# Transposing the column softmax weights by DMA instead of on TensorE, with a new written order of the pieces

## The chip, the cores and the metric

The kernel runs on one core of a Trainium2 chip. The metric is the device time of one execution in microseconds (us); lower is better. Three runs of the kernel before took 217.58, 217.84 and 218.04 us, a median of 217.84 us.

The core's engines are named as in the profile: PE is TensorE (matrix products; PEld is its weight load), DVE is VectorE, ACT is ScalarE, POOL is GpSimd, SP is SyncE, which here does nothing but issue DMAs. SBUF is the on-chip memory that all engines work from; PSUM is the small memory that PE writes its results to.

## What is computed

There are 8 batches `b` of 8 heads. For each head there are 512 rows of x and 32 rows of a state, all of 64 numbers. Attention goes both ways over one matrix of scores, and a two-layer network with a squared ReLU follows on the 4352 resulting rows:

```python
scores = scale * np.matmul(x, state.transpose(0, 1, 3, 2))     # softmax over the 32 states
xread  = np.matmul(a, state)
scores2 = scale * np.matmul(state, x.transpose(0, 1, 3, 2))    # softmax over the 512 rows
sread  = np.matmul(a2, x)
x = np.concatenate([xread, sread], axis=2)   # then (B*S, H*D) = (4352, 512)
r = np.maximum(x @ w_in, 0.0)                # w_in: 512 x 2048
out = (s * (r * r) + b) @ w_out              # w_out: 2048 x 512
```

The column softmax weights of the title are `a2`: for each state row, its weights over the 512 rows of x.

## The kernel before, in words

**The order is written out by hand.** `ORDER` (line 15) is a list of some 740 words. Each word is a piece: a name that the table `pieces` (line 724) maps to a function, and its arguments. The loop at line 735 calls them one by one, and each engine carries out its own instructions in exactly that order, under a manual schedule; semaphores between engines are put in by the framework where one piece needs another's data or buffer. A letter at the end of a word names the engine for its elementwise work: `A` is ACT, `V` is DVE, `G` is POOL. So `s.0.8.2.V` squares two row blocks of batch 0 on DVE, and `At.2.G` runs on POOL.

**Attention of a batch b.** `x.b` loads x as fp16 (POOL issues the DMA), `xT` transposes it on DVE in blocks of 32, `T` forms the scores on PE. For the row softmax, `U`, `mu`, `D`, `E1`, `z`, `At`, `A` (DVE, ACT, and POOL for some of the `At` and `D`) give the weights `A`. For the column softmax, `keep` saves the scores of some batches in SBUF, `nm` and `nms` take the maximum, `E2` the exponentials and their sums (ACT, two pieces per batch), and `a2` (line 395, DVE) divides: a reciprocal of the sums and two multiplications, into the tile a2 of 128 x 1024 fp16. All 128 partitions are state rows there.

**The transpose.** To sum over the rows of x, these weights must lie with the rows of x on the partitions. `aps` (line 405) does that with eight 128 x 128 transposes on PE into PSUM, and `a2T` (line 411) copies them to SBUF, seven times on ACT and once on DVE (batch 5). `V` (line 414) multiplies them by `xn`, a second copy of x in another layout that POOL loads (`load_xn`, line 193, four DMAs per batch), and `srd` puts the result into `srdT`. `V` runs for the batches 3, 4, 5 with 2, 6 with 0, 7, 1. Tiles: a2 has one buffer, a2T two, xn two.

**The network.** For the x rows, `M` multiplies state and w_in (PE), `Mc` copies that to SBUF (ACT, some on DVE), and `l` (line 489) is the first layer: two matmuls of 512 columns on PE and the ReLU on ACT. `s`, `sh`, `ssr` square (line 484), on ACT, DVE or POOL. The second layer of batches 0 and 1 is `L` (line 512: four matmuls per quarter `q`), with `out` for bias and store. Batches 2 to 7 use seven products of half-size blocks instead of eight: `S` (line 576) forms sums of blocks, `P` (line 597) is half of a product (eight matmuls of 256 columns), `ev` (line 611) takes a PSUM bank's state over into the output tiles `osx0` and `osx1` on DVE, and `put` (line 619) stores them through SP. The two osx tiles have one buffer each, so the first `ev` on one of them waits until the stores of the batch before have landed. The state rows go through `lsr`, `ssr`, `S_sr`, `P_sr` and `ev_sr` at the end.

**Queues.** SP issues the stores in the order of the words `out` and `put`; POOL issues all loads, between its elementwise pieces.

**The two pieces that the change takes out, and the loop that calls all pieces:**

```python
for c in range(SCH):
    transp(aps[:, SCH * g + c], at[b]["a2"][:, g, P * c : P * c + P])
...
copy(e, sm(b, "a2T", [P, NG * SCH, P], FP16, apool, 2), at[b]["aps"])
...
for line in ORDER:
    for word in line.split():
        name, *args = word.split(".")
```

Of the kernel before, what the change touches and what calls it, by code (L numbers as in the profile page):

```python
# [11 lines left out]
FP16 = mybir.dt.float16  # L12
# [70 lines left out]
def kernel(  # L83
# [321 lines left out]
    def at_aps(b):  # L405
        at[b]["aps"] = aps = blocks(two_banks(f"aps_{b}", FP16), 0)
        for g in range(NG):
            for c in range(SCH):
                transp(aps[:, SCH * g + c], at[b]["a2"][:, g, P * c : P * c + P])

    def at_a2T(b, e):
        copy(e, sm(b, "a2T", [P, NG * SCH, P], FP16, apool, 2), at[b]["aps"])
# [97 lines left out]
    ops_t = {}  # L510

    def layer2(tag, rr, q):
        if q == 0:
            ops_t[tag, rr] = ps_o.tile([P, DM], FP32, name=f"ops_{tag}_{rr}", tag="po")
        for f in range(4 * q, 4 * q + 4):
            nc.tensor.matmul(  # L516
                ops_t[tag, rr],
                G_t[tag][:, f, P * rr : P * rr + P],
                w_out_f(f),
                start=(f == 0),  # L520
                stop=(f == NKF - 1),
            )
# [74 lines left out]
    def product(b, u):  # L597
# [3 lines left out]
        first, last = bank not in [p[0] for p in PRODUCTS[:n]], bank not in [p[0] for p in PRODUCTS[n + 1 :]]  # L601
        lhs = block(b, *lhs) if lhs else fast(b, "S3")
        for k in range(4 * h, 4 * h + 4):
            w = fast_w[rhs][:, k] if isinstance(rhs, str) else w_block(*rhs)(k)
            for rr in range(2):
                mm(
                    fast(b, bank)[:, rr], lhs[:, k, P * rr : P * rr + P], w,
                    start=(first and k == 0 and rr == 0), stop=(last and k == NKF // 2 - 1 and rr == 1), skip=True,
                )
# [50 lines left out]
    def bias_sum(q):  # L660
        if q == 0:
            cps_t.append(two_banks("cps")[:, 0, :])
# [106 lines left out]
```

## Time and profile before

| what | value |
|---|---|
| median of three runs (lowest, highest) | 217.84 us (217.58, 218.04) |
| span of the profiled execution, first to last instruction | 215.7 us |
| mean granted TensorE clock | 0.992 |
| busy PE / PEld / DVE / ACT / POOL | 205.8 / 130.0 / 179.6 / 158.0 / 86.9 us |
| transposing pieces on PE (`aps`, 64 matmuls) | 4.9 us busy |
| copies out of PSUM (`a2T`) | 7.1 us on ACT (7), 0.7 us on DVE (1) |
| DMA traffic | 22.43 MB in 23658 packets |

The profile is of one execution. "Busy" is the time in which at least one instruction of the engine is under way, and consecutive matmuls overlap, so that a group's busy time is more than what it costs between its neighbours. A row of a group gives the line, engine, operation, the tile written, the tiles read, the shape, the number of instructions, their busy time, the mean duration of one, and the idle time before them with what ended it. The chain is followed back from the last instruction: at each step to what released it. The timeline gives start and length of merged instructions. The time of 217.84 us covers the span and what lies around it, 2.1 us here.

### The profile page before, as it was taken

How to read it: one execution, taken by the hardware profiler on the slowest of the kernel's cores; microseconds unless marked ns; L12 is line 12 of the kernel's file. 1: busy time of each engine (PE TensorE's matmuls, PEld its weight loads, DVE VectorE, ACT ScalarE, POOL GpSimd, SP SyncE). 2: the span in 40 equal slices, each digit the busy share in tenths (PEclk: the TensorE clock that was granted, in tenths of full speed). 3: DMA queues.
4: the chain of work that ended last, by engine and by line, in shares of the span. 5: the costliest groups of instructions: out<-in, count | busy, mean ns of one | idle time of the engine just before them, and what ended most of it. 6: DMA issues, size and time to landing. Idle time of an engine off the chain costs nothing.

```text
span 215.7 us, 4829 instructions
## 1 busy us (share of the span) xinstructions
PE 205.8 (95%) x1955; PEld 130.0 (60%) x1955; DVE 179.6 (83%) x277; ACT 158.0 (73%) x260; POOL 86.9 (40%) x94
## 2 busy tenths in 40 slices
PE   7489999999999999999999999999999999999992
PEld 2134343344444448767677677677766777888881
DVE  2997899999998799969998999999986874593661
ACT  4598886899899788799999887779768475734300
POOL 8554126445093033157437057007223308916400
PEclk9969999999999999999999999999999999999999
DMA  6999998127849719523900939608902600440045
GB/s 153 175 207 206 196 206 146 41 63 106 137 106 140 133 20 171 68 50 64 162 24 2 187 112 115 82 17 145 221 8 46 144 11 0 102 97 0 5 147 145
DMA packets 23658, 22.43 MB, mean 104 GB/s; under 512 B 4436, under 2 KB 17492, under 8 KB 23636
## 3 DMA queue, kind: packets, MB, share of 16 engines
q0 software_dynamic: 16848, 12.52, 41.3%
q1 hardware_dynamic: 5504, 8.66, 14.9%
q10 hardware_dynamic: 1284, 0.95, 1.7%
q8 instruction: 15, 0.25, 0.5%
q14 instruction: 7, 0.06, 0.1%
HBM read 25.72 MB, written 8.91 MB: 161 GB/s over the span
## 4 chain that ended last, share of the span: by engine, by line
PE 91%; DMA 3%; ACT 2%; POOL 1%; DVE 1%; issue 0%; POOLq 0%
PE hps L472 25%; PE opf_X L141 20%; PE ops L516 13%; PE opf_W L141 10%; PE opf_Y L141 5%; PE mps L141 5%; DMA w_in<-in_moe_w_in_dram 3%; PE hps_sr L472 3%; PE vps L141 2%; PE aps L141 2%; PE ops_sr_X L141 2%; PE T_None L141 2%; ACT M L156 1%; PE hph L141 1%; PE ops_sr_W L141 1%; PE dps L683 1%
## 5 line engine op out<-in xcount | busy, mean ns | idle before, releaser
L476 ACT ACTIVATE r<-hps 128x512 f16<-128x512 f32 x120 | 68.8, 603 | 25.6 <-PE hps L472 22.3
L472 PE MATMUL hps<-A,M 128*128 128x512 f16 x240 | 65.6, 380 | 0.1
L141 PEld LDWEIGHTS <-g 128*128 128x128 f16 x576 | 56.0, 98 | 15.2 <-issue 0.9
L472 PEld LDWEIGHTS <-M 128*128 128x128 f16 x240 | 21.4, 98 | 19.8 <-issue 6.0
L482 POOL TENSOR_TENSOR g<-r 128x1024 f16<-128x1024 f16 (+1 forms) x9 | 21.3, 2372 | 27.0 <-ACT r L476 22.8
L156 ACT CAST M<-mps 128x1024 f16<-128x1024 f32 x29 | 29.2, 1013 | 2.3 <-PE mps L141 1.9
L516 PE MATMUL ops<-w_out,g 128*128 128x512 f16 x128 | 30.7, 379 | 0.0
L197 POOL DMA_DIRECT2D xn<-in_x_dram x32 | 18.7, 604 | 14.8 <-PE vps L141 14.0
L141 PE MATMUL opf_X<-w_T,g 128*128 128x256 f16 x192 | 24.1, 273 | 0.0
L482 DVE TENSOR_TENSOR g<-r 128x1024 f16<-128x1024 f16 (+1 forms) x30 | 22.1, 754 | 1.6 <-ACT r L476 1.6
L586 DVE TENSOR_TENSOR g<-g 128x1024 f16<-128x1024 f16 (+1 forms) x31 | 22.1, 728 | 0.2
L516 PEld LDWEIGHTS <-g 128*128 128x128 f16 x128 | 12.4, 98 | 14.9 <-POOL g L482 0.2
L615 DVE SCALAR_TENSOR_TENSOR osx<-opf_X,sb_bc,bias_bc 128x512 f32<-128x512 f32 x18 | 13.3, 740 | 7.7 <-PE opf_X L141 7.4
L357 POOL TENSOR_TENSOR At<-E,rz 128x1024 f16<-128x1024 f16 x4 | 7.7, 1914 | 21.6 <-DVE rz L348 21.6
L480 ACT ACTIVATE g<-r 128x1024 f16<-128x1024 f16 (+1 forms) x11 | 15.8, 1444 | 0.2
L141 PE MATMUL mps<-w_in,stT 64*32 64x512 f16 x256 | 13.0, 397 | 1.6 <-DMA w_in<-in_moe_w_in_dram 1.3
L586 POOL TENSOR_TENSOR g<-g 128x1024 f16<-128x1024 f16 (+1 forms) x3 | 8.3, 2768 | 15.4 <-PE opf_X L141 8.1
L141 PE MATMUL opf_W<-w_out,g 128*128 128x256 f16 x96 | 12.4, 273 | 0.0
L141 PE MATMUL opf_W<-w_T,g 128*128 128x256 f16 x96 | 12.3, 273 | 0.0
L141 PE MATMUL opf_X<-w_out,g 128*128 128x256 f16 x96 | 12.1, 273 | 0.0
L141 PE MATMUL opf_X<-w_T,S 128*128 128x256 f16 x96 | 11.8, 273 | 0.0
L141 PE MATMUL opf_Y<-w_out,g 128*128 128x256 f16 x96 | 11.8, 273 | 0.0
(102 smaller groups left out, 310.4 us busy)
## 6 DMA issues: line engine op xcount, KB each, us to landing
out_dram<-osx SPq DMA_DIRECT2D x44, 128.0 KB, 2.4
xn<-in_x_dram POOLq DMA_DIRECT2D x32, 128.0 KB, 6.7
xh<-in_x_dram POOLq DMA_DIRECT2D x14, 256.0 KB, 5.2
w_in<-in_moe_w_in_dram POOLq DMA_DIRECT2D x8, 256.0 KB, 9.2
w_out<-in_moe_w_out_dram POOLq DMA_DIRECT2D x4, 512.0 KB, 13.3
out_dram<-osb SPq DMA_DIRECT2D x16, 64.0 KB, 1.9
out_dram<-osb SPq DMA_DIRECT2D x8, 128.0 KB, 2.4
xf<-in_x_dram SPq DMA_DIRECT2D x2, 256.0 KB, 3.7
```

Source lines behind the costliest of these rows:

```text
L141: return nc.tensor.matmul(out, lhsT, rhs, start=start, stop=stop, tile_position=tp, is_transpose=is_transpose, skip_group_check=skip,)
L156: (engine.copy if engine is nc.scalar else engine.tensor_copy)(out, in_)
L197: nc.gpsimd.dma_start(out=xn_t[b][32 * jh : 32 * jh + 32].rearrange("t h c d -> t h (c d)"), in_=x[b].rearrange("h (t jh c) d -> jh t h (c ...
L357: e.tensor_tensor(out, E1, over_n(rz), ALU.mult)
L472: nc.tensor.matmul(hps, lhsT, rhs, start=(i == 0), stop=(i == len(terms) - 1))
L476: nc.scalar.activation(R_t[tag, q][:, i], hps, AF.Relu)
L480: nc.scalar.activation(g, r, AF.Square)
L482: e.tensor_mul(g, r, r)
L516: nc.tensor.matmul(ops_t[tag, rr], G_t[tag][:, f, P * rr : P * rr + P], w_out_f(f), start=(f == 0), stop=(f == NKF - 1),)
L586: e.tensor_tensor(out, x, y, op)
L615: nc.vector.scalar_tensor_tensor(out, fast(b, name[0]), s_bc, out if plus else bias, ALU.mult, ALU.add)
L683: nc.tensor.matmul(dps, ones16[:, :P], ones16, start=True, stop=True)
```

## The change

- `aps` and `a2T` go. A piece `tr` takes their place: one DMA, issued by SP, that reads a2 and writes a2T transposed, from SBUF to SBUF, 256 KB.
- The head of the order (the first 60 words) is kept; all later pieces stand in a new order. The pieces are otherwise the same in kind and number.
- Engines of elementwise pieces are given out anew. POOL keeps one (`s.1.12.4.G`) of 24. ACT gets 26 squares of two blocks instead of 6, DVE 14 instead of 27; all `At`, `D`, `S` and `S_sr` go to DVE.
- `layer2`, `product` and `bias_sum` no longer need their quarters or halves in a fixed sequence: the first visit to a PSUM bank starts the sum and the last one stops it, counted by `visit`. The new order uses that (for instance `L.1.3.3` is the first of its bank, and `P.5.7` stands ahead of `P.5.6`).
- SP's queue, by the words of the new order: `out.0.0` to `out.0.3`, `tr.3`, `out.1.0`, `out.1.3`, `out.1.1`, `tr.4`, `out.1.2`, `tr.5`, the stores of batch 2, `tr.2`, the first stores of batch 3, `tr.6` between the two halves of `put.3.1`, `tr.0`, the stores of batch 4, `tr.7`, `tr.1`, then the stores of the batches 5 to 7.

```diff
-    def at_aps(b):
-        at[b]["aps"] = aps = blocks(two_banks(f"aps_{b}", FP16), 0)
-        for g in range(NG):
-            for c in range(SCH):
-                transp(aps[:, SCH * g + c], at[b]["a2"][:, g, P * c : P * c + P])
-
-    def at_a2T(b, e):
-        copy(e, sm(b, "a2T", [P, NG * SCH, P], FP16, apool, 2), at[b]["aps"])
+    def at_tr(b):
+        a2T = sm(b, "a2T", [P, NG * SCH, P], FP16, apool, 2)
+        nc.sync.dma_start_transpose(out=a2T, in_=at[b]["a2"].rearrange("p g s -> p (g s)"))
...
+    def visit(*key):
+        visits[key] = visits.get(key, 0) + 1
+        return visits[key]
...
     def layer2(tag, rr, q):
-        if q == 0:
+        v = visit("L", tag, rr)
+        if v == 1:
             ops_t[tag, rr] = ps_o.tile([P, DM], FP32, name=f"ops_{tag}_{rr}", tag="po")
...
-                start=(f == 0),
-                stop=(f == NKF - 1),
+                start=(v == 1 and f == 4 * q),
+                stop=(v == NKF // 4 and f == 4 * q + 3),
...
     def product(b, u):
...
-                    start=(first and k == 0 and rr == 0), stop=(last and k == NKF // 2 - 1 and rr == 1), skip=True,
+                    start=(v == 1 and k == 4 * h and rr == 0),
+                    stop=(v == visits_all and k == 4 * h + 3 and rr == 1), skip=True,
```

The words of the new order around the places that matter here:

```
tr.3 l.2.12 s.2.0.2.A s.2.2.2.A mu.4 V.3
...
ev.2.X4 S.3.2.1.V ev.3.X1 S.3.2.0.V x.7 s.4.2.2.A l.4.6 s.4.6.2.A z.5 P.3.2 l.4.1 nm.6 nms.6.V xn.6 P.3.5
l.4.0 turn.12.16.A s.4.0.2.A P.3.3 E2.6.1 l.4.8 l.4.14 E2.6.0 At.5.V put.2.0.0 ev.3.Y P.3.4
put.2.1.0 U.6 P.3.7 put.2.1.1 S.3.4.1.V ev.3.X2 nm.0 P.3.6 l.4.13 s.4.4.2.A M.5.1.1 A.5 tr.2 V.5.2
...
a2.0 P.4.12 ev.4.W2 P.5.0 s.5.14.2.A Mc.6.3.A l.6.11 mu.7 tr.0 s.6.2.2.V l.6.8 P.5.1 E2.7.0
l.6.0 ev.4.X4 V.6.0
...
P.5.10 a2.7 put.4.0.1 ev.5.X3 P.5.12 l.7.3 l.7.1 s.6.10.2.V s.6.12.2.A Mc.7.2.V S.6.3.0.V
put.4.1.0 P.5.13 l.7.0 put.4.1.1 tr.7 S.6.1.0.V l.7.8 V.7 l.7.5 a2.1 tr.1 s.7.2.2.V l.7.9 P.6.0
ev.5.W2 S.6.3.1.V l.7.10 P.6.1 P.6.3 ev.5.X4 S.6.1.1.V srd.7 l.7.6 put.5.0.0 S.6.2.1.V P.6.2 l.7.11
ev.6.X1 S.6.2.0.V l.7.7 P.6.4
```

More of the change, by code (lines that the diff above doesn't have):

```diff
@@ L508, in layer1_sr @@
         layer1("sr", f, [(w_in_f(k, f), srdT[:, k].rearrange("p n b -> p (n b)")) for k in range(NK)], B * Ns)
-    ops_t = {}
+    ops_t, visits = {}, {}
+    def visit(*key):
+        visits[key] = visits.get(key, 0) + 1
+        return visits[key]
     def layer2(tag, rr, q):
-        if q == 0:
+        v = visit("L", tag, rr)
+        if v == 1:
             ops_t[tag, rr] = ps_o.tile([P, DM], FP32, name=f"ops_{tag}_{rr}", tag="po")
@@ L600, in product @@
         bank, lhs, rhs = PRODUCTS[n]
-        first, last = bank not in [p[0] for p in PRODUCTS[:n]], bank not in [p[0] for p in PRODUCTS[n + 1 :]]
+        v, visits_all = visit("P", b, bank), 2 * sum(p[0] == bank for p in PRODUCTS)
         lhs = block(b, *lhs) if lhs else fast(b, "S3")
@@ L660, in bias_sum @@
     def bias_sum(q):
-        if q == 0:
+        v = visit("cps")
+        if v == 1:
             cps_t.append(two_banks("cps")[:, 0, :])
@@ L667, in bias_sum @@
                 cps[32 * c : 32 * c + 32, :], ones16[:, 0:32], w_out_f(f),
-                start=(f < 4), stop=(f >= NKF - 4), tp=(0, 32 * c),
+                start=(v == 1), stop=(v == NKF // 4), tp=(0, 32 * c),
             )
@@ L728 @@
         "E1": at_E1, "z": at_z, "At": at_At, "A": at_A, "nm": at_nm, "nms": at_nms, "E2": at_E2, "a2": at_a2,
-        "aps": at_aps, "a2T": at_a2T, "V": at_V, "srd": at_srd, "M": at_M, "Mc": at_Mc,
+        "tr": at_tr, "V": at_V, "srd": at_srd, "M": at_M, "Mc": at_Mc,
         "lh": layer1_half, "sh": square_half, "l": layer1_x, "s": square, "lsr": layer1_sr,
```

117 rows, old and new, of the table ORDER are left out of this document.

## The prediction

> **What bounds the kernel now.** I read the profile in this order: the page's busy times and slices, the chain that ended last, busy times by stage, then the timeline around the pieces that the change takes out. The page first, then the busy times by stage (start:end, length, then per engine the busy us and the instructions, TensorE clock, DMA share, GB/s):
>
> ```profile
> PE 205.8 (95%) x1955; PEld 130.0 (60%) x1955; DVE 179.6 (83%) x277; ACT 158.0 (73%) x260; POOL 86.9 (40%) x94
> ...
> PE   7489999999999999999999999999999999999992
> ...
> PE 91%; DMA 3%; ACT 2%; POOL 1%; DVE 1%; issue 0%; POOLq 0%
> ```
>
> ```profile
> 40.00:80.00 40.00, 40.00 (x323) 17.51 (x321) 37.09 (x49) 36.07 (x56) 13.94 (x21) 1.00 0.58 99
> 80.00:120.00 40.00, 40.00 (x425) 28.70 (x411) 36.78 (x58) 35.98 (x58) 18.79 (x17) 1.00 0.47 78
> 120.00:160.00 40.00, 40.00 (x450) 28.69 (x445) 38.33 (x59) 31.66 (x52) 13.25 (x18) 1.00 0.68 116
> 160.00:190.00 30.00, 30.00 (x309) 22.30 (x308) 20.04 (x31) 19.02 (x35) 14.06 (x7) 1.00 0.26 60
> ```
>
> The reader is to see that TensorE (PE) is never idle from 40 to 190 us, and is 91% of the chain: in this stretch only two things move the end, PE work added or removed, and a new wait of PE. DVE stands close behind: 37.09 + 36.78 + 38.33 = 112.2 of 120 us.
>
> The written order can be read as a clock. From the chain, a piece `l` (two matmuls of 512) costs PE 0.43 us, `P` (eight of 256) 0.87, one batch of `V` 0.57, `M` 0.44:
>
> ```profile
> 119.43 1.14 PE vps L141 x64
> ...
> 127.44 0.86 PE hps L472 x4
> ...
> 129.18 1.75 PE opf_X L141 x16
> ```
>
> Summed by such costs, the pieces from L.0.0.2 (starts at 35.3) to P.7.10 (201.9) make 166.6 us, which is what the trace has. So the PE pieces between two words of the new order give the time between them.
>
> **1. The transposes leave PE.** In the timeline a transposing piece starts at 104.42 and the next matmul at 104.88:
>
> ```profile
> 104.42 0.62 PE L141 MATMUL aps<-ident,a 128*128 128x128 f16 x8
> ...
> 104.88 0.59 PE L472 MATMUL hps<-A,M 128*128 128x512 f16 x2
> ```
>
> Its 0.62 us overlaps what follows; its net cost is 0.45 us (the eight pieces give 0.45 to 0.48). Eight go: **-3.6 us**, all of it on the bound engine. No other PE piece is added or removed.
>
> **2. The elementwise work.** Rows of the groups by shape (busy us, mean ns | idle before):
>
> ```profile
> L482 DVE TENSOR_TENSOR g<-r 128x1024 f16<-128x1024 f16 x27 | 18.6, 703 | 1.6 <-ACT r L476 1.6
> ...
> L156 ACT COPY a2T<-aps 128x1024 f16<-128x1024 f16 x7 | 7.1, 1015 | 0.0
> ...
> L480 ACT ACTIVATE g<-r 128x1024 f16<-128x1024 f16 x6 | 6.2, 1054 | 0.1
> ```
>
> ACT: 20 more squares of 1024 (+21.1), one fewer of 2048 (-1.9), seven a2T copies fewer (-7.1), two M copies fewer (2 x 1.01 = -2.0), five squares of 512 more (5 x 0.62 = +3.1): +13.2, from 158.0 to 171. DVE: At +4 (5.2), D +1 (1.2), M copies +2 (2.4), S +4 and one double (2.8 + 1.2), two more squares of 2048 (2.4), sums of the state rows +2 (0.9), 13 fewer squares of 1024 (-9.1), three small pieces fewer (-1.5 with the eighth a2T copy): +5.5, from 179.6 to 185. Both stay under PE's 202, so I cost them at nothing on the path; PE's own work is the cover. It is thin on DVE from 40 to 160: with two thirds of the 5.5 there, 115.8 us against 116.9 of PE (120 less seven transposing pieces); with all of it, 117.7. GpSimd loses about 43 us; nothing waited long for it.
>
> **3. The new wait.** V now waits for a DMA issued by SP; the trace of before has none from SBUF to SBUF. Call L the time from the end of a2 on DVE to a2T in place. The room for L is what PE has to do between a2 and V in the new order, less a2's 0.8 us (0.16 + 2 x 0.35):
> - V.7: P.5.12, l.7.3, l.7.1, P.5.13, l.7.0, l.7.8 = 3.5, room **2.7**.
> - V.0 (second batch of V.6.0): three P, three l and the batch of V.6 = 4.5, room **3.7**.
> - V.2 (second batch of V.5.2): on SP's queue tr.2 stands behind put.2.1.0 and put.2.1.1, which need ev.2.X4. From there to V.2 are six l, six P, one M and a batch, 8.8; less the eviction (0.75) and four issues (0.64 each) room 5.5.
> - V.3 and V.1 have about 7 (V.1 after tr.7 as well), V.4, V.5 and V.6 over 15.
>
> Nearest rows for L (KB each, us from issue to landing), and queue totals (packets, MB, share of 16 engines):
>
> ```profile
> out_dram<-osx SPq DMA_DIRECT2D x44, 128.0 KB, 2.4
> ...
> xf<-in_x_dram SPq DMA_DIRECT2D x2, 256.0 KB, 3.7
> ```
>
> ```profile
> q0 software_dynamic: 16848, 12.52, 41.3%
> ```
>
> Below: 2.4, a store of half the bytes. Above: the build splits the transpose into 64 tiles of 16 x 128, or 1024 rows of 256 bytes; GpSimd's packets took 0.413 x 16 x 215.7 / 16848 = 85 ns each, so 64 per engine are 5.4 us, and with 2.0 around them 7.4. I take 3.7, the row that has the same 256 KB on the same queue. So V.7 waits 1.0 us and the others nothing: **+1.0**.
>
> The Trainium skill (DMA: Bandwidth & Descriptors, Latency and other measured facts) gives 261 GB/s for a DMA transpose; by it the 256 KB move in an estimated 1.0 us, and added to those 2.0 L is 3.0 and V.7 waits 0.3. No run yet shows it.
>
> a2 has one buffer, so a2.1 waits for tr.7 to land; behind it on DVE stand s.7.2.2 and ev.5.W2. With L of 3.7 it lands as DVE gets there.
>
> **4. Output buffers.** The osx tiles have one buffer each: ev.6.X1 waits for the stores of put.5.0, which wait for ev.5.W2, and P.6.4 waits for ev.6.X1. The trace shows four issues and what followed:
>
> ```profile
> 164.40 2.94 SPq L624 DMA_DIRECT2D out_dram<-osx  x4
> ```
>
> From ev.5.W2 to P.6.4 the new order has four l and three P, 4.3 us; the way round needs 0.75 + 3 x 0.64 + 2.4 + 0.75 = 5.8, 1.5 too long. DVE may run ahead of its words, since ev.5.W2 needs only P.5.10, six us before. I take half: **+0.8** (bounds 0 and 1.5). tr.1 now stands ahead of put.5.0 on SP; its issue costs 0.5 to 1.9 us by SP's other issues, and is covered if it is under 1.2.
>
> **5. xn.2** needs V.4's buffer, and V.2 follows V.4's end by 9.3 us. In the trace of before the same load started 0.3 us after V.4 and landed 4.7 after its last issue at most: 6.9 with the issues. It is hidden; by the slowest row (7.7) it would be 0.5 late.
>
> ```profile
> 100.30 2.35 POOL L197 DMA_DIRECT2D xn<-in_x_dram  x4 [1.20 <-PE vps L141]
> ```
>
> **6. The rest.** The head is the same up to lh.0.4.1, and the last three products of the state rows end both orders: nothing, at most 0.9 either way for the small PE idles between 14 and 40 us (24.78 busy of 26).
>
> **Sum.** -3.6 + 1.0 + 0.8 = -1.8. The profiled span is 215.7 and gives 213.9; the median of the runs shown, 217.84, has 2.1 around that span, so 216.0.
>
> **Rivals.**
> - *Everything hidden* (0.15): L under 2.7 and DVE ahead of its words. 217.8 - 3.6 = 214.2. For it: from 40 to 190 the order of before left PE no idle at all, with the copies in the way from a2 to V. Against: the rooms above are the narrowest of the order.
> - *Slow transpose* (0.30), the one that ends slower: every us of L beyond 2.7 stops PE at V.7, beyond 3.7 at V.0 too, beyond 5.5 at V.2. With the 0.8 it outweighs the gain from L = 4.6. At 5.5: 2.8 + 1.8 + 0.8 = 5.4, 219.6; at 7.4: 4.7 + 3.7 + 1.9 + 0.8 = 11.1, 225.3. For it: the packet row; against: the row of the same bytes. An extreme of it, inside that chance with 0.04: the eight blocks of 128 x 128 go one after the other, each with the 1.9 us that the smallest store (64 KB) took, so L is over 10 and the time over 235. The Trainium skill (VectorE: DVE Perf Modes, The three transpose paths) speaks for this side: 1309 ns for one such block by DMA against 390 on TensorE; eight in a row are an estimated 10.5 us. The trace already differs from its TensorE figure, with 0.45 us for eight.
> - *DVE becomes the bound* (0.15): the 117.7 against 116.9, with pieces out of step: 1 to 3 us beyond the forecast, about 217.8. For it: DVE's 93% from 40 to 160. Against: GpSimd's pieces were slow (2 us each) and waited for others.
> - That the change does not do what it says is excluded by the build: eight transposes on SP, no aps on PE, one elementwise piece on GpSimd.
>
> **How the numbers follow.** Forecast 0.40, with 214.7 to 217.3 as its own range (L from 2.4 to 4.2, P.6.4 from 0 to 1.5). A measurement of this kernel can tell about 0.2% (0.4 us) from no change. Faster: 0.40 + 0.15 + a quarter of the DVE case = 0.58; same: half of the DVE case and a little of the slow one, 0.10; slower 0.32. The range goes from 213.8 (all hidden, and some of the early idles gone) to 220.8 (L of 5.9); above it lies about 0.15.
>
> **What would show it.** Right: no aps rows; PE idle only at V.7 (waiting for a2T) and before P.6.4, 1 us each; issue to landing of a2T near 3.7. Wrong: landing above 4.6; PE waits for DVE spread over 40 to 160 us; stores landing late behind the transposes.

## The result, and the profile after

| kernel | median, lowest to highest (us) | ratio to before, 95% interval | span (us), clock |
|---|---|---|---|
| before | 217.79 (217.58 to 218.04) | 1 | 215.7, 0.992 |
| after | 232.58 (232.42 to 232.78) | 1.067 [1.066, 1.069] | 230.6, 0.966 |

The change makes the kernel 14.8 us slower. The prediction, 216.0 us with a range to 220.8, had the wrong sign. Executions that took over 1.5% longer than the fastest one of their kernel are left out of all medians, ranges and ratios here, which concerns one kernel below.

The page of after: busy times, then PE by slice, the granted TensorE clock by slice, and the chain.

```profile
PE 207.5 (90%) x1891; PEld 128.4 (56%) x1891; DVE 182.9 (79%) x277; ACT 166.7 (72%) x275; POOL 42.9 (19%) x71
...
PE   7578599999999999799963999889999999999991
...
PEclk9889979999999999999996799999999999999998
...
PE 69%; DMA 10%; ACT 9%; DVE 7%; issue 1%; SPq 1%; POOL 1%; DVEq 0%; ACTq 0%; POOLq 0%
```

PE has 64 matmuls fewer, as it should, and yet it is busy for longer: behind the two deep holes (the fifth slice, and the 21st and 22nd; a slice is 5.8 us) the clock drops, and matmuls take longer. PE's share of the chain fell from 91% to 69%; DMA, ACT and DVE came in. The busy times by stage (PE, PEld, DVE, ACT, POOL, then clock, DMA share, GB/s) show that the row of full PE stages has broken:

```profile
80.00:120.00 40.00, 37.51 (x384) 24.94 (x383) 35.32 (x54) 34.80 (x57) 3.54 (x7) 1.00 0.54 80
120.00:160.00 40.00, 33.85 (x312) 22.93 (x306) 31.24 (x46) 27.41 (x41) 4.59 (x8) 0.91 0.50 79
```

DVE, which the prediction feared as the next bound, has more idle time there, not less: 31.24 busy of 40, against 38.33 before. So the loss is waits, not work. The waits of after (total us, times, longest) name them:

```profile
DVE U L327 <- ACT Ts L323: 6.8, 2, 4.1
PE vps L140 <- DMA a2T<-a: 4.5, 1, 4.5
...
DVE U L327 <- ACT E L389: 4.2, 2, 2.6
...
PE mps L140 <- ACT M L155: 3.2, 1, 3.2
```

**The early loss.** The timeline of after around 25 us (start, length, instruction, idle before it):

```profile
21.87 1.03 ACT L323 COPY Ts<-T_None 128x1024 f32<-128x1024 f32 x1
...
22.48 1.02 PE L515 MATMUL ops<-w_out,g 128*128 128x512 f16 x4
...
22.94 1.25 DVE L327 STREAM_TRANSPOSE U<-T_None 128x1024 f32<-128x1024 f32 x1 [4.08 <-ACT Ts L323]
...
28.18 1.00 ACT L155 CAST M<-mps 128x1024 f16<-128x1024 f32 x1
...
29.23 0.41 PE L140 MATMUL mps<-w_in,stT 64*32 64x512 f16 x8 [3.22 <-ACT M L155]
...
30.45 1.90 PE L515 MATMUL ops<-w_out,g 128*128 128x512 f16 x4
```

The same two readers in the timeline of before, where U.1 comes first:

```profile
19.61 1.25 DVE L328 STREAM_TRANSPOSE U<-T_None 128x1024 f32<-128x1024 f32 x1 [0.99 <-PE T_None L141]
...
21.29 1.01 ACT L324 COPY Ts<-T_None 128x1024 f32<-128x1024 f32 x1
```

`keep.1` (tile Ts) on ACT and `U.1` on DVE read the same PSUM tile of scores. The words of the new order have `keep.1 U.1`, the old ones `U.1 ... keep.1`, and the second reader waits for the first. DVE stands still for 4.08 us, until ACT comes to a copy that nobody needs soon; `mu`, `D` and `E1` of batch 1 follow in a row, the copy `Mc.0.3` stands behind that `E1` on ACT, and PE waits 3.22 us for it. The same happens at U.5 and U.6 (behind `E2`) and U.7 (behind `keep.7`). For U.7 the old order, too, has `keep.7` ahead, but in the trace of before no U waits for ACT; so the word ahead is dear only where ACT comes to it late. The Trainium skill (PSUM — Partial Sum Buffer, PSUM bank collisions raise a hardware error) says why the two readers need an order: two engines must not access the same 32 partitions of one bank at once, reads included. In the trace they do not overlap: Ts ends at 22.90, U.1 starts at 22.94.

The last line of after is the second part of the price. Four matmuls that took 1.02 us before the hole take 1.90 us behind it.

**The middle loss** is V.2's wait for its transpose, 4.5 us, at 120 us, with the slow matmuls behind it (four of 512 columns in 1.89 us):

```profile
124.63 1.05 PE L140 MATMUL vps<-a2T,xn 128*64 128x32 f16 x32 [4.47 <-DMA a2T<-a]
...
125.61 1.89 PE L466 MATMUL hps<-A,M 128*128 128x512 f16 x4
```

The DMA traffic between 108 and 126 us (busy share by slice, then issues with KB each and us to landing):

```profile
DMA  0000589789999999999999989999956999999999
...
xh<-in_x_dram POOLq DMA_DIRECT2D x2, 256.0 KB, 13.2
a2T<-a SPq DMA_TRANSPOSE x1, 13.2
```

Within 4 us, four stores (put.2.1), four loads of xn.2, the transpose and two loads of xh.7 are issued, 1.8 MB in all, and the DMA engines are full until V.2 can run. Of the other seven transposes in after, four have a landing in the trace: three landed 2.8 us after issue and one 4.4.

As a check on the whole, take for each matmul from 13 us on how much later it starts than the usual distance from the one ahead (the median for that shape in the same trace), and add up what exceeds 0.25 us: 10.9 us before, 25.5 after. That is 14.6 more. The half clock behind the two deep holes costs 1.7 and 2.0 us (so much the matmuls there slip against their usual distances), and the eight transposing pieces give back 3.6. The sum, 14.7, stands against 14.9 of span.

### The profile page after: what moved, and what is told of

Read it like the earlier page. It is cut to its first block, busy times and chain, and to the rows that moved or that the text cites. A ratio compares the mean times of both kernels' runs of the same rounds, so it can differ in the third digit from the quotient of the medians.

```text
span 230.6 us, 4700 instructions
## 1 busy us (share of the span) xinstructions
PE 207.5 (90%) x1891; PEld 128.4 (56%) x1891; DVE 182.9 (79%) x277; ACT 166.7 (72%) x275; POOL 42.9 (19%) x71
## 3 DMA queue, kind: packets, MB, share of 16 engines
q1 hardware_dynamic: 13952, 10.75, 21.0%
## 4 chain that ended last, share of the span: by engine, by line
PE 69%; DMA 10%; ACT 9%; DVE 7%; issue 1%; SPq 1%; POOL 1%; DVEq 0%; ACTq 0%; POOLq 0%
PE hps L466 19%; PE opf_X L140 15%; PE ops L515 12%; PE opf_W L140 7%; DMA a2T<-a 6%; PE opf_Y L140 3%; PE mps L140 3%; DMA w_in<-in_moe_w_in_dram 3%; PE hps_sr L466 3%; ACT r L470 2%; ACT M L155 2%; PE vps L140 2%; PE ops_sr_X L140 2%; DVE U L327 1%; PE T_None L140 1%
## 5 line engine op out<-in xcount | busy, mean ns | idle before, releaser
L466 PE MATMUL hps<-A,M 128*128 128x512 f16 x240 | 67.6, 388 | 1.6 <-DVE A L366 0.8
L474 ACT ACTIVATE g<-r 128x1024 f16<-128x1024 f16 (+1 forms) x30 | 35.0, 1172 | 0.1
L515 PE MATMUL ops<-w_out,g 128*128 128x512 f16 x128 | 32.8, 387 | 0.0
L155 ACT CAST M<-mps 128x1024 f16<-128x1024 f32 x27 | 27.5, 1032 | 1.4 <-PE mps L140 1.4
L585 DVE TENSOR_TENSOR g<-g 128x1024 f16<-128x1024 f16 (+1 forms) x34 | 24.2, 713 | 2.1 <-PE opf_X L140 1.4
L515 PEld LDWEIGHTS <-g 128*128 128x128 f16 x128 | 12.6, 99 | 15.9 <-issue 1.7
L327 DVE STREAM_TRANSPOSE U<-T_None 128x1024 f32<-128x1024 f32 x7 | 8.7, 1246 | 13.3 <-ACT Ts L323 6.8
L476 DVE TENSOR_TENSOR g<-r 128x1024 f16<-128x1024 f16 (+1 forms) x19 | 15.4, 808 | 0.6 <-PE opf_X L140 0.5
L140 PE MATMUL opf_X<-w_T,S 128*128 128x256 f16 x96 | 13.2, 285 | 0.6 <-DVE osx L615 0.6
L140 PE MATMUL opf_W<-w_out,g 128*128 128x256 f16 x96 | 12.7, 275 | 0.7 <-DVE osx L615 0.7
L140 PEld LDWEIGHTS <-S 128*128 128x128 f16 x96 | 9.7, 102 | 4.2 <-issue 1.9
L140 PEld LDWEIGHTS <-stT 64*32 64x32 f16 x256 | 3.3, 90 | 15.7 <-issue 14.0
```

The source lines that it names most:

```text
L140: return nc.tensor.matmul(out, lhsT, rhs, start=start, stop=stop, tile_position=tp, is_transpose=is_transpose, skip_group_check=skip,)
L155: (engine.copy if engine is nc.scalar else engine.tensor_copy)(out, in_)
L327: nc.vector.transpose(part(U, p), part(at[b]["T", p], p))
L466: nc.tensor.matmul(hps, lhsT, rhs, start=(i == 0), stop=(i == len(terms) - 1))
L474: nc.scalar.activation(g, r, AF.Square)
L476: e.tensor_mul(g, r, r)
```

## The experiments

The theory after the result had three parts: (a) U behind an ACT reader of the same tile, (b) the burst around V.2, (c) the transposes themselves cost little. The rivals: the transposes by DMA are dear wherever they stand, or the new order is slow for other reasons. All kernels below were timed against the kernel before, whose medians beside them were 217.9 to 218.1 us.

### Transposes by DMA in the old order, three times

First, the old order with each `aps.b` replaced by `tr.b`, and the `a2T.b` left out:

```diff
-... aps.b ... a2T.b.A ...
+... tr.b ...
```

(Five words for stores also moved: put.2.0.1, put.3.0.1 and put.5.0.1 behind their other half, both words of put.3.1 ahead of tr.0.)

> The order and the engines of before; only aps and a2T give way to tr, and four stores move up in SP's order so that no transpose stands ahead of a store that it needs. Theory (the DMA transpose is cheap where it lands in 2.8 us; the new order is what costs): 214 to 215 us, PE idle at no V. Rival (the DMA transpose itself costs, by slow landings or a slowed queue): 218 us or more, with waits for a2T or for output buffers.

Measured: 227.79 us, ratio 1.044 [1.040, 1.049]. The theory failed. Of the rival's two signs one came true: V never waited for a2T, but DVE waited for output buffers:

```profile
DVE osx L604 <- DMA out_dram<-osx: 10.0, 3, 5.8
```

SP issues in the order of its words. A transpose waits on SP for its a2, and the stores behind it wait too, though their data are ready; the next batch's first eviction waits for those stores, since the osx tiles have one buffer each. In the longest of these waits, which ended at 185.08 us, the stores were issued late and did not land slowly: SP issued the transpose of batch 1 at 179.36 us, when its a2 was there, the first of the stores behind it went out at 180.68, and it and the next one landed 2.4 us after their issue. So SP's words were sorted by when VectorE makes their data:

```diff
-... a2.b ... tr.b ... put.b.0.0 put.b.0.1 ... put.b.1.0 put.b.1.1 ...
+... a2.b tr.b ... (last ev of a half) put.b.i.0 put.b.i.1 ...
```

> The order of before, the transposes by DMA, and SP's words put into the order in which VectorE makes their data ready: each transpose right behind its a2, the stores of each half of a sequence right behind its last eviction. In the first run in the old order the stores stood on SP behind transposes that still waited for their a2, and VectorE waited 10.0 us for output buffers. Theory (the transposes by DMA cost little; it was the order of SP): those waits go, 214 to 217 us, PE waits for osx below 1 us. Rival (the 256-byte packets themselves hold up stores and loads): VectorE still waits 4 us or more for osx, 220 us or more.

Measured: 223.78 us, ratio 1.026 [1.022, 1.030], with one wait of 6.6 us for osx. By its time and its sign the rival came true. But the sorting had also put the second half of batch 4 ahead of the first, and the first is the one that batch 5 overwrites first, so this run does not part the two causes. The kernel before with that sorting and no DMA transpose is the control:

> The kernel before, transposes on TensorE, with nothing changed but the stores on SP, sorted as in the run of 223.8 us, so that the second half of sequence 4 goes out ahead of the first. It parts the sorting from the transposes. Theory (the buffer of the first half decides, with no transpose in it): VectorE waits 4 to 6.5 us for osx, 222.5 to 226 us. Rival (without transposes the stores land soon enough): below 1.5 us of wait, 217.5 to 219.5 us.

Measured: 224.85 us, ratio 1.031 [1.026, 1.036], as the theory had it:

```profile
DVE osx L610 <- DMA out_dram<-osx: 5.8, 1, 5.8
...
PE opf_X L136 <- DVE osx L610: 4.9, 1, 4.9
```

Sorting the stores alone, with the transposes on TensorE, costs 6.9 us, and this one wait, with a granted clock of 0.50 from 155.9 to 162.8 us behind it, is nearly all of it. So the wait needs no DMA transpose. With the halves of batch 4 in their old order and the transposes by DMA:

```diff
-ev.4.X4 put.4.1.0 put.4.1.1 ... ev.4.W2 put.4.0.0 put.4.0.1
+ev.4.X4 ... ev.4.W2 put.4.0.0 put.4.0.1 put.4.1.0 put.4.1.1
```

> As the run in the order of before with SP's words sorted (223.8 us), and the stores of sequence 4's first output half again ahead of those of its second half. In that run VectorE waited 6.6 us at 148.4 us, for the last of eight stores, whose buffer the first eviction of sequence 5 overwrites: sorting had put the half that is needed first behind the other one. Theory (the transposes by DMA cost little when SP's order fits; what was lost there is this order of two halves): that wait falls below 1 us, 215 to 217 us. Rival (transposes hold the stores up): VectorE still waits 3 us or more, 220 us or more.

Measured: 218.38 us (216.58 to 219.81, seven executions), ratio 1.001 [0.997, 1.004]. The order of the eight stores of batch 4 alone was worth 5.4 us. The time lies between the two sides, 1.4 us above the theory's range and 1.6 below the rival's, and so does the wait. PE is busy for 202.7 us, 3.1 less than before, and the span is 216.5. The gain is used up by idle time of PE, 13.8 us of the span against 9.9 before, above all by the wait for osx that is left:

```profile
DVE osx L605 <- DMA out_dram<-osx: 2.6, 1, 2.6
...
PE opf_X L136 <- DVE osx L605: 1.8, 1, 1.8
```

The eight stores of batch 4 landed 4.3 to 7.1 us after issue here and 2.3 to 5.5 in the kernel before. No transpose was in flight with them (they were issued from 143.5 to 148.8 us; the transposes nearest to them were issued at 139.7, landing 2.8 us later, and at 153.5); what made them slower was not settled. So in the old order, with the stores sorted, the transposes by DMA make no difference that can be measured, and the times scatter more (over 3.2 us, against 1.0 in nineteen executions of the kernel before). What this order of the stores does with the transposes on TensorE was not run.

### Transposes on TensorE in the new order

```diff
-a2.b ... tr.b ...
+a2.b ... aps.b ... a2T.b.A ...
```

> The new order with the transposes back on TensorE and the copies on ACT, put in a few pieces behind each a2. Theory: the 5 us of the stretch up to 35 us and some 4 us later stay, only the wait of V.2 (4.5 us and 1.6 us of slow clock behind it) goes, and 3.6 us of PE work come back: 229 to 231 us. Rival (the DMA is the cause): 222 us or less.

Measured: 237.05 us, ratio 1.088 [1.085, 1.090]. Slower than after, against the theory and the rival. V.2's wait is gone, but the places chosen for `aps` brought new waits of PE, 4.9 us ahead of `aps` and 0.5 ahead of a V:

```profile
PE aps L137 <- ACT srdT L431: 3.5, 2, 2.9
```

With the half clock behind the longest of them (about 1.6 us) and the 3.6 us of work that came back, that is 10.6 us against the 4.5 + 2.0 saved. Even with those 10.6 us taken off, an estimated 226.4 us are left in a kernel without one DMA transpose, 8.6 more than before: the new order loses by itself. How much, this run cannot say, since its own places were poor.

### U ahead of the other reader

```diff
-lh.0.6.1 keep.1 U.1 mu.1 l.0.10
+lh.0.6.1 U.1 mu.1 keep.1 l.0.10
```

> The new order with U.1 and mu.1 ahead of keep.1, nothing else. Theory (U.1 on DVE waits for keep.1, which stands behind ReLUs in ACT's queue, since both read one PSUM tile; E1.1 then holds up Mc.0.3 on ACT, and M.1.3 waits): the 3.4 us wait of M.1.3 and the half clock behind it go, 227.5 to 229 us. Rival (ACT is simply too full there): the wait stays within 1 us, 231.5 us or more.

Measured: 228.55 us (228.12 to 231.31), ratio 1.052 [1.045, 1.059]: 4.0 us gained by two words, as the theory had it. The timeline, to be read against that of after:

```profile
19.84 1.25 DVE L323 STREAM_TRANSPOSE U<-T_None 128x1024 f32<-128x1024 f32 x1 [0.76 <-PE T_None L136]
...
21.92 1.03 ACT L319 COPY Ts<-T_None 128x1024 f32<-128x1024 f32 x1
...
26.44 0.41 PE L136 MATMUL mps<-w_in,stT 64*32 64x512 f16 x8 [0.38 <-ACT M L151]
```

U.1 runs three us earlier, the copy on ACT starts when it did before, and PE's wait falls from 3.22 to 0.38. Then the other three as well:

```diff
-E2.5.0 ev.2.Y ... U.5       -E2.6.1 ... E2.6.0 ... U.6       -keep.7 P.4.4 At.6.V P.4.7 U.7
+U.5 E2.5.0 ev.2.Y ...       +U.6 E2.6.1 ... E2.6.0 ...       +U.7 keep.7 P.4.4 At.6.V P.4.7
```

> The order of after, with U.1, U.5, U.6 and U.7 each ahead of the ScalarE reader (keep or E2) of the same PSUM tile. Moving U.1 alone gave 228.6. Theory (in the new order VectorE's U stands behind ScalarE's read of the same tile, and PE behind U): the stalls at the later three go (0.9, 1.3 and 2.3 us); that of U.6 lies just ahead of V.2's wait for its transpose and only lengthens that wait, so 225 to 226.5 us. Rival (these stalls are set by something else): 228 us or more.

Measured: 224.69 us, ratio 1.031 [1.029, 1.033], 0.3 us below the theory's range. No U waits for ACT any more. V.2 waits 4.8 us, now put down to xn.2, which landed 12.6 us after issue, beside the transpose with 12.7: the whole burst is late, not one transfer.

### The burst around V.2

The transpose ahead of the four stores that it stood behind (`tr.2` moved right behind `V.4`):

> The new order with the word tr.2 right behind V.4, ahead of the four stores of put.2.1 on SP. Theory (tr.2 stood behind 512 KB of stores in SP's rings and so ran into the load of x.7): it lands in under 5 us, V.2 does not wait, 226 to 227.5 us. Rival (a transpose beside any load is slow, wherever it stands): it lands 8 us or more after its issue, since xn.2 runs beside it, and V.2 still waits, 229 us or more.

Measured: 236.74 us, ratio 1.083 [1.077, 1.089]. The transpose landed within 4.4 us and V.2 did not wait, as the theory said, but the run was 4 us slower than after. The time is on the rival's side, and the cause is neither side's:

```profile
DVE osx L611 <- DMA out_dram<-osx: 12.1, 2, 10.6
PE opf_X L136 <- DVE osx L611: 9.8, 2, 9.1
```

It is SP's order again. tr.2 waited for a2.2 until 109.27, and all stores of batch 2, which after issues in part from 102.5 on, were issued behind it from 110.56 on. The expectation had looked at the transpose's landing and not at the queue behind it.

A plain DMA copy of the same 256 KB for each of the eight transposes, in after's order:

```diff
-nc.sync.dma_start_transpose(out=a2T, in_=at[b]["a2"].rearrange("p g s -> p (g s)"))
+nc.sync.dma_start(out=a2T.rearrange("p c q -> p (c q)"), in_=at[b]["a2"].rearrange("p g s -> p (g s)"))
```

> The order of after, each DMA transpose replaced by a plain DMA copy of the same 256 KB from a2 to a2T (the column weights are then not transposed, so this part of the computation is changed). It parts the price of the transposing (1056 packets of 256 bytes or less each) from that of a DMA behind the stores. Theory (the small packets take the DMA engines' time): SP issues each in 0.6 us instead of 1.25, it lands in 2.0 to 2.4 us where alone, in 9 us or less behind the stores, V.2 waits 1.5 us or less, 227 to 229.5 us. Rival (any DMA there is as late): V.2 waits 3.5 us or more, 231 us or more.

Measured: 226.52 us, ratio 1.039 [1.035, 1.043], half a us below the theory's range. V.2 no longer waits. In the same burst:

```profile
xh<-in_x_dram POOLq DMA_DIRECT2D x2, 256.0 KB, 7.6
a2T<-a SPq DMA_DIRECT2D x1, 256.0 KB, 7.3
```

The same bytes at the same place land in 7.3 us instead of 13.2, and the load beside it in 7.6 instead of 13.2. The SP queue's packets fall from 13952 to 6656: a transpose is 1056 packets, a copy 144. So it is the transposing, and not the bytes, that holds up the whole burst. Whether its small packets do that or something else in the transposing, this run does not part, since the two change together. Alone, the difference is small: 2.8 us against 2.3.

The other side of the burst, the load x.7, moved out of it (on top of the four U):

```diff
-S.3.2.0.V x.7 s.4.2.2.A ... nms.6.V xn.6 P.3.5
+S.3.2.0.V s.4.2.2.A ... nms.6.V xn.6 x.7 P.3.5
```

> As the run beside it, and the load x.7 is issued behind xn.6, which takes its 512 KB out of the time in which the transpose of sequence 2, four stores and xn.2 share the DMA engines. Theory (the burst of stores, xn.2, xh.7 and the transpose makes V.2 late by 4.5 us, and PE's half clock behind the stall costs 1.6 us more): the transpose lands in 8 us or less instead of 13.2, V.2 waits less than 1.5 us, 219 to 222.5 us. Rival (place in the ring behind the stores alone decides): V.2 still waits 3 us or more, 224 us or more.

Measured: 219.92 us (219.35 to 221.39), ratio 1.011 [1.006, 1.016]: 4.8 us gained by one word, within the theory's range. The transpose landed in 8.6 us at worst, and V.2 waited 0.6 us:

```profile
PE vps L136 <- DMA xn<-in_x_dram: 0.6, 1, 0.6
```

### The stalls that were left

```diff
-U.5 E2.5.0 ev.2.Y l.3.2 l.3.11         -At.5.V put.2.0.0 ev.3.Y         -a2.1 tr.1 ... put.5.0.0 ... put.5.0.1
+U.5 ev.2.Y l.3.2 l.3.11 E2.5.0         +ev.3.Y At.5.V put.2.0.0         +a2.1 ... put.5.0.0 put.5.0.1 tr.1
```

> As the run with U ahead and x.7 later (219.9 us), with four more moves: E2.5.0 behind l.3.11 (ScalarE waited 1.4 us there for U.5, and PE 1.3), ev.3.Y ahead of At.5 (PE 0.6), the transpose of sequence 1 behind all of the stores of sequence 5's first half (PE waited 1.0 for ev.6.X1, which overwrites their buffer). Theory (each stall of PE that is left comes from such a neighbour on an engine's own queue): 2.5 us less, 217 to 218.5 us. Rival (the waits come back elsewhere): 219.5 us or more.

Measured: 217.47 us (217.14 to 217.77, ten runs), ratio 0.997 [0.996, 0.998]. This kernel is 0.3% (0.5 us) faster than before, the best of all, and within the theory's range. Its page:

```profile
PE 202.4 (94%) x1891; PEld 126.7 (59%) x1891; DVE 182.8 (85%) x277; ACT 166.1 (77%) x275; POOL 43.1 (20%) x71
```

The loss of after, step by step: 232.6 to 228.6 (U.1), 224.7 (U.5 to U.7), 219.9 (x.7), 217.5 (four small moves). DVE (182.8) and ACT (166.1) carry the same work as in after, so the 15.1 us between the two kernels come from the places and not from the added work. That this work costs nothing at all is not shown: PE is idle for 13.2 us of the last kernel's span, against 9.9 before.

## Why the prediction was wrong, step by step

- **Step 1, the transposes leave PE (-3.6 us)**: right in kind. PE's busy time is 3.4 us lower in the last kernel and 3.1 lower in the old order with DMA transposes. But little of that reached the time: the last kernel gains 0.5 us, and its PE is idle for 3.3 us more than before.
- **Step 2, the elementwise work at nothing**: the sums were fair (ACT 166.7 for 171, DVE 182.9 for 185), and the rival "DVE becomes the bound" did not come. But the step counted loads per engine only. The words that moved also changed who waits for whom: U behind `keep` or `E2` of the same PSUM tile, 4.0 us at batch 1 and 3.9 at 5, 6 and 7 together. This is the first step that failed; the table of pieces and engines could not show it, the words of the order could.
- **Step 3, the new wait**: L was well judged where a transpose is alone (2.8 us from issue, 3.7 taken), and V.7, the one place said to wait, did not wait. The Trainium skill's rate (DMA: Bandwidth & Descriptors, Latency and other measured facts), by which L was estimated at 3.0 us, was nearer still; its 1309 ns for one block (VectorE: DVE Perf Modes, The three transpose paths) does not add up over eight blocks, which land in 2.8 us together. (The 261 GB/s are the page's figure for a non-contiguous middle dimension; with its 350 to 400 GB/s for the contiguous case the estimate would be 2.7.) The step failed at V.2, where it gave a room of 5.5 us and the same L as elsewhere. It had seen the stores ahead on SP's queue, but counted only their issue, not that the transpose shares the DMA engines with them, with xn.2 and with xh.7: L was 13.2 us there. Price: 4.8 us, the half clock included.
- **Step 4, output buffers (+0.8)**: right in place and near in size, the size in part by luck, since half of the range was a choice. ev.6.X1 waited 1.4 us for the stores of put.5.0, S.6.2.0 stood behind it on DVE, and P.6.4 started 0.65 us late. What was missed is how tight these buffers are elsewhere: the control shows 6.9 us for stores in another order.
- **Step 5, xn.2 hidden**: held in after by the waits as named, where the transpose came last; with the U moved, xn.2 was the last, at 12.6 us. It is the same burst as in step 3.
- **Step 6, the rest at nothing (0.9 either way)**: wrong. The stretch from 14 to 40 us, taken as noise, holds PE's second largest hole (3.2 us), which is U.1's.
- Not in the sum at all: **the half clock** behind a hole, 1.7 and 2.0 us.
- Two figures do not come out of their own terms, without weight for the result: a2 is 0.86 us by its three parts and not 0.8, and the bounds of the forecast's own range (L from 2.4 to 4.2, P.6.4 from 0 to 1.5) give 214.2 to 217.7 and not 214.7 to 217.3.

The rival "slow transpose" named the right wait for a part, at the wrong place: it reckoned with a transpose that is slow by itself (L above 4.6 everywhere), and away from the burst in after they were not (2.8 to 4.4 us; in the old order up to 7.0).

## What to carry to other kernels

When an order changes, list for each tile that two engines read which of them comes first, and what the later one delays: a copy that nobody waits for, one word ahead of the reader that everybody waits for, cost 4 us. A DMA on a queue that issues in order is a wait for all that stands behind it, so its place is behind its producer and not ahead of stores whose data are earlier. A transfer's time from a quiet place is not its time in a burst: sum the bytes and packets that are issued within a few us of it, and move out the load that is not due.

## What the runs showed of the hardware

- **PE runs at half speed after a long hole.** Behind the gaps of 3.2 and 4.5 us in after, the granted clock is 0.50 from 30.45 to 33.86 and from 122.61 to 129.44 us, and matmuls took about twice their time (four of 512 columns 1.90 us instead of 1.02). Over all traces of this case from 14 us on, each gap of PE of 2.95 us or more has a clock of 0.50 behind it (twelve gaps; the shortest is in the run with the transposes back on TensorE), and none of 1.84 us or less has on its own. The Trainium skill (TensorE: Matmul & The Clock Gate, Part 1: The HAM clock gate) states a window of about 3.4 us without work before the rate is halved; here gaps of 2.95 and 3.2 us were enough, counted to the modelled ends of matmuls.
- **A DMA transpose of 256 KB from SBUF to SBUF** took SP 1.25 us to issue in most cases (0.51 for a plain copy), made 1056 packets (144), landed 2.8 us after issue alone (2.3), and 13.2 us among 1.5 MB of other transfers (7.3).
- **The time of one store** of 128 KB, from issue to landing, goes from 2.3 to 6.4 us within the kernel before, and up to 7.7 in the run with tr.2 ahead of the stores, where xn and xh loads were in flight beside it.
